# Where the conversions of w2 stand in the queues: raw slices fetched two mixing steps sooner, conversions at even distances

## The chip, the core and the metric

The kernel runs on one core of one Trainium2 chip. The time is the device time of one execution in microseconds, and the median of several runs is what is compared. A core has engines that each run their own queue of instructions in order: TensorE (PE, with PEld for its weight loads), VectorE (DVE), ScalarE (ACT), GpSimd (POOL), and SyncE (SP), which only issues transfers here.

## What is computed

The reference is an attention block, whose output goes through a Fourier mixing block:

```python
# attention: 4 batches, 8 heads, 768 tokens, head size 64
q_bucket = sum of (q @ proj > 0) bits times powers of two      # 6 bits
k_bucket = the same of k
scores = q @ k^T / 8, where q_bucket == k_bucket, else -1e9
attn = softmax(scores) @ v
# bridge: x[b, s, h*64 + d], 4 x 768 x 512
mixed = real(fft(fft(x, axis=1), axis=2))
u  = x + mixed
un = (u - mean(u)) / sqrt(var(u) + 1e-6)
out = u + relu(un @ w_ch1) @ w_ch2          # 512 -> 2048 -> 512
```

The two weight matrices come as 64-bit floats. The kernel fetches them as raw 64-bit words and makes 32-bit floats of them itself: for w_ch2 (w2 below) this is the conversion that the change moves.

## The kernel before

**Stages.** For each batch b the loop at line 1536 interleaves two generators. `attention(b)` yields once for each of its 24 chunks (4 pairs of heads, 6 chunks of 128 keys). `other` is `mix(b-1)`, the Fourier mixing and the two-layer network (`mlp7`) of the batch before, in steps that are handed out evenly between the chunks. So in the second round (b = 1) the mixing and network of batch 0 run beside the attention of batch 1.

**Attention, per chunk.** TensorE makes scores of two heads (`scores`, L894). ScalarE takes the exponential (`weights`, L905) into one of two buffers pk0 and pk1. VectorE multiplies by the bucket mask (`weigh`, L919, one instruction for each head). TensorE multiplies by the values (`values`, L930); VectorE adds the chunk into a running sum (L1007). At a pair's end come the reciprocal of the sum and the scaling (`scale`, L941 to L970). The next pair is prepared in between (`prepare`: L768, L825, L829, L839, L849).

**Mixing.** `fold`, then products with cosine and sine tables (L1122, copied by ScalarE at L1129 and L1135), then products A and B (L1151) that VectorE adds into x (L1165).

**Network.** Both layers use a scheme of seven products for eight. `quarters(f)` forms four sums and differences of a quarter of w1 in the tile tq on VectorE (L1224 to L1227) and stores the parts to DRAM (`ad`, L1229 and L1230, on SyncE) for the later batches. `inner` runs the seven products of each of eight f (TensorE, L1426); each product's bank goes through a ScalarE copy (L1448, L1451, L1458, L1463, L1467, L1475) or an activation, and a VectorE addition (L1452, L1459, L1464, L1468, L1476). Two halves of four f each are followed by a down-projection each (`outer7`, L1306).

**Conversion of w2.** w2 comes in 16 slices of 512 KB. `weights2` (L1249) fetches and converts them. There are two buffers for raw slices, in a tile (`zraw2`) that takes the place of the mixing's z. `Arrival.fetch` issues a transfer on GpSimd's queue (L693). `Arrival.convert` calls `narrow`, and then fetches the slice after next. One conversion is L639 and L643 on VectorE, L647 on ScalarE (these read the raw slice), the additions (L649, shown as L652 in the profile) on VectorE, and L654 and L655 on ScalarE, which record unusual values. After every second conversion VectorE makes four differences (L1272 to L1275). The finished half is stored to DRAM (`bd`, L1277, on SyncE).

**What sets the order.** The first round is recorded in the order written (`manual_schedule`, L1517). After it, a scheduler places the instructions on each engine's queue. It takes the traced order as priority, together with what it holds to be ready when; a `behind()` block pins some matmuls behind others. Where a conversion is called in the generators is therefore a wish, and its place in each queue is the scheduler's. A queue is run in order: an instruction that waits for a transfer holds all behind it on the same engine.

**Where the conversions are called.** `after(n, one, two)` (L1499) advances `weights2` in three of five steps of `mix(0)` from step 8 on (L1582). In the second half `mlp7` advances it at L1487 in three of four steps.

Of the kernel before, what the change touches and what calls it, by code (L numbers as in the profile page):

```python
# [17 lines left out]
ALU = mybir.AluOpType  # L18
# [467 lines left out]
def _main(  # L486
# [188 lines left out]
    def centre(f, avg):  # L675
        for c in range(NDC):
            w = w1[:, c, f : f + WC]
            nc.vector.tensor_tensor(w, w, avg, op=ALU.subtract)

    class Arrival:  # L680

# [221 lines left out]
    def weights(pk, g, ps):  # L903

        nc.scalar.activation(  # L905
            pk[:, g, :, 0:HALF], ps[:, :, 0:HALF], AF.Exp, scale=SCALE
        )

    def weigh(n, c, pss):

        qb, kb = preps[n][2:]
        pk = pks[npk[0] % NPK]
        npk[0] += 1
        for g in range(2) if n >= TWO else ():
            weights(pk, g, pss[g])
        if kb is not None:
            for h in range(2):
                w = pk[:, :, h, 0:HALF]
                nc.vector.scalar_tensor_tensor(  # L919
                    w, qb[:, h].rearrange("p (g s) -> p g s", g=2), kb[:, h, c : c + 1], w,  # L920
                    op0=ALU.is_equal, op1=ALU.mult,
                )
        return pk
# [181 lines left out]
    def mix(b):  # L1105
# [8 lines left out]
        for par in range(2):  # L1114
            for t in range(NT // 2):
# [12 lines left out]
                for k in kinds:  # L1128
                    nc.scalar.copy(  # L1129
                        f[:, k, k : hd + 1 - k],  # L1130
                        ps[:, k * (hd + 1) : DM if k else hd + 1],
                    )
# [12 lines left out]
        for j in range(NDC):  # L1145
# [10 lines left out]
            for ps, op in (pa, ALU.add), (pb, ALU.subtract):  # L1156
                for i in range(2):
# [4 lines left out]
                    else:  # L1162
                        f = ps[:, HW : HALF + 1]
                        f = bass.AP(f.tensor, f.offset, [f.ap[0], [HW, 2], [-1, HW]])
                    nc.vector.tensor_tensor(  # L1165
                        u, u, f, op=op if (j < 2) ^ i else ALU.add
# [82 lines left out]
    def weights2():  # L1249
# [14 lines left out]
        for half in range(2):  # L1264
            for i in range(arrival.depth) if half == 0 else ():
                arrival.fetch(i)
            for i in range(HF):
                arrival.convert(half * HF + i)
                yield
# [99 lines left out]
    def mlp7(b):  # L1369
# [7 lines left out]
        if b == 0:  # L1377
# [11 lines left out]
            ss = [s1s[0], spare[3].rearrange("p (r n) -> p r n", n=P)]  # L1389
            quarters(0)  # L1390
        prods = [A11, S2, A12, S1, S3, S4, A22]
# [41 lines left out]
        def inner(half):  # L1433
            for r in range(HF // 2):
# [15 lines left out]
                product(S2, p6)  # L1450
                nc.scalar.copy(c21, p6)  # L1451
                nc.vector.tensor_tensor(c21, c12, c21, op=ALU.add)  # L1452
                yield
# [3 lines left out]
                product(S1, p5)  # L1457
                nc.scalar.copy(c22, p5)  # L1458
                nc.vector.tensor_tensor(c22, c21, c22, op=ALU.add)  # L1459
                yield  # L1460
# [6 lines left out]
                nc.scalar.copy(c12, p5)  # L1467
                nc.vector.tensor_tensor(c12, c21, c12, op=ALU.add)  # L1468
                nc.scalar.activation(c12, c12, AF.Relu)
                if b and f == 0:  # L1470
# [4 lines left out]
                nc.scalar.copy(sd[1], p7)  # L1475
                nc.vector.tensor_tensor(c21, c21, sd[1], op=ALU.add)  # L1476
                nc.scalar.activation(c21, c21, AF.Relu)
                if b == 0 and r < HF // 2 - 1:
# [36 lines left out]

    ET = mybir.EngineType
    with tc.manual_schedule(engines={ET.PE, ET.DVE, ET.Activation, ET.Pool, ET.SP}):  # L1517
# [18 lines left out]
    for b in range(B):  # L1536
# [93 lines left out]
```

## Time and profile before

| what | value |
|---|---|
| median of 3 runs | 1095.56 us (1094.76 to 1096.2) |
| the profiled execution's own time | 1097.14 us |
| its span | 1095.2 us |
| TensorE busy | 1036.7 us, 95% |
| VectorE busy | 789.0 us, 72% |
| ScalarE busy | 500.1 us, 46% |
| GpSimd busy | 58.3 us, 5% |
| fetches of raw slices of w2 | 16, from 151.2 to 337.5 us |
| conversions of w2 on VectorE | from 155.8 to 346.9 us |

Times in the profile count from the span's start. In a timeline, a row is a start, a duration, engine, line, operation, tiles and shapes, and in brackets the idle time before it and what ended it. The rows overlap a little, as the engines are pipelined, so the distance from one start to the next is what an instruction takes in a row of its like. In the list of waits, the three numbers are the total, the number of times and the longest, in us.

### The profile page before, as it was taken

The numbers are of one execution on the slowest core, as the hardware profiler recorded it, in microseconds if no ns is written. First come the engines' busy times: TensorE is split into PE (matmuls) and PEld (weight loads), VectorE is DVE, ScalarE is ACT, GpSimd is POOL, SyncE is SP. The second block draws the span as 40 slices with busy tenths as digits, with TensorE's granted clock in tenths as the row PEclk, the third lists the DMA queues.
The fourth block names the chain that finished last, engine by engine and source line by source line (L and its number), as shares of the span: only waits on it lengthen the run. The fifth ranks groups of instructions, "written<-read, shape, count | busy, mean of one in ns | idle before, by whom it ended". The sixth has DMA issues, their size and how long they took to land.

```text
span 1095.2 us, 14139 instructions
## 1 busy us (share of the span) xinstructions
PE 1036.7 (95%) x4933; PEld 634.0 (58%) x4933; DVE 789.0 (72%) x1336; ACT 500.1 (46%) x1055; POOL 58.3 (5%) x132
## 2 busy tenths in 40 slices
PE   6989897999989999999999999999999999999997
PEld 3333354446744675545674576645675569768676
DVE  5899968868599978694867776876775875744353
ACT  6988555653276325364426423354415522341430
POOL 0000000002000020010000011001000002100000
PEclk9999899999999999999999999999999999999999
DMA  8744363441056162214063224213123204122401
GB/s 222 225 91 97 60 166 85 149 148 26 20 138 200 55 199 56 51 54 92 15 176 90 63 54 168 44 34 90 27 71 122 78 20 173 52 85 71 141 20 41
DMA packets 175710, 103.13 MB, mean 94 GB/s; under 512 B 129552, under 2 KB 162960, under 8 KB 175632
## 3 DMA queue, kind: packets, MB, share of 16 engines
q1 hardware_dynamic: 169840, 88.65, 30.1%
q0 software_dynamic: 4224, 13.11, 3.8%
q8 instruction: 41, 0.67, 0.3%
q10 hardware_dynamic: 1568, 0.39, 0.2%
q14 instruction: 37, 0.30, 0.1%
HBM read 81.14 MB, written 20.97 MB: 93 GB/s over the span
## 4 chain that ended last, share of the span: by engine, by line
PE 57%; DVE 15%; ACT 4%; issue 3%; DMA 2%; DVEq 0%; ACTq 0%
PE o L1306 23%; PE h_p L1426 18%; PE oo L930 5%; PE sc L894 5%; DVE pk L919 5%; DVE acc L1007 3%; PE cs L1122 2%; DMA zraw<-in_moe_w_ch_dram 2%; PE A L1151 1%; ACT rr L965 1%; ACT pk L905 1%; PE B L1151 1%; PE bits L825 1%; DVE x L1165 1%; DVE w L1318 0%
## 5 line engine op out<-in xcount | busy, mean ns | idle before, releaser
L1306 PE MATMUL o<-w,h 128*128 128x256 f32 x1152 | 258.5, 381 | 1.9 <-DVE w L1318 0.8
L1306 PEld LDWEIGHTS o<-w,h 128*128 128x128 f32 x1152 | 216.8, 190 | 41.7 <-issue 3.5
L905 ACT ACTIVATE pk<-sc 128x768 f32<-128x768 f32 x192 | 146.9, 809 | 94.2 <-PE sc L894 31.3
L1426 PE MATMUL h_p<-x,w 128*128 128x384 f32 x448 | 162.4, 492 | 2.1 <-ACT h L1448 1.7
L894 PE MATMUL sc<-qt,kt 64*128 64x384 f32 x768 | 154.2, 504 | 6.2 <-ACT pk L905 5.9
L919 DVE SCALAR_TENSOR_TENSOR pk<-qb,kb,pk 128x768 f32<-128x768 bf16 x132 | 129.3, 1012 | 34.5 <-ACT pk L905 34.3
L930 PE MATMUL oo<-pk,vn 128*64 128x385 f32 (+1 forms) x768 | 147.8, 495 | 4.9 <-DVE pk L919 4.6
L1426 PEld LDWEIGHTS h_p<-x,w 128*128 128x128 f32 x448 | 82.5, 190 | 67.2 <-issue 6.8
L1007 DVE TENSOR_TENSOR acc<-acc,pk 128x1536 f32<-128x1536 f32 (+1 forms) x72 | 105.9, 1484 | 5.9 <-ACT pk L905 5.4
L1426 PE MATMUL h_p<-w 128*128 128x384 f32 x288 | 106.3, 492 | 3.6 <-ACT w L1463 2.3
L930 PEld LDWEIGHTS oo<-pk,vn 128*64 128x64 f32 x768 | 50.7, 136 | 92.3 <-issue 73.3
L894 PEld LDWEIGHTS sc<-qt,kt 64*128 64x128 f32 x768 | 66.6, 187 | 57.4 <-issue 19.0
L1426 PEld LDWEIGHTS h_p<-w 128*128 128x128 f32 x288 | 53.0, 190 | 45.5 <-ACT w L1475 5.1
L1318 DVE SCALAR_TENSOR_TENSOR w<-o,rs,w 128x256 f32<-128x256 f32 x56 | 26.7, 479 | 42.0 <-PE o L1306 42.0
L1336 ACT COPY tq<-o 128x256 f32<-128x256 f32 x24 | 8.9, 373 | 101.8 <-PE o L1306 101.8
L1306 PE MATMUL o<-w 128*128 128x256 f32 x176 | 42.0, 381 | 0.3 <-DVE w L1318 0.3
L1459 DVE TENSOR_TENSOR h<-h 128x384 f32<-128x384 f32 x32 | 17.7, 553 | 29.5 <-ACT h L1458 29.5
L1452 DVE TENSOR_TENSOR h<-h 128x384 f32<-128x384 f32 x32 | 17.8, 555 | 26.9 <-ACT h L1451 26.8
L1306 PEld LDWEIGHTS o<-w 128*128 128x128 f32 x176 | 33.0, 190 | 6.8 <-issue 1.1
L1060 POOL DMA_DIRECT2D out_dram<-w x30 | 16.4, 548 | 376.0 <-ACT tq L1336 146.3
L1325 ACT COPY tq<-o 128x256 f32<-128x256 f32 x24 | 8.9, 370 | 58.4 <-PE o L1306 58.3
L1352 DVE TENSOR_TENSOR tq<-tq,o 128x256 f32<-128x256 f32 x24 | 10.0, 418 | 33.7 <-PE o L1306 33.7
(170 smaller groups left out, 1339.1 us busy)
## 6 DMA issues: line engine op xcount, KB each, us to landing
w<-ad SPq DMA_DIRECT2D x168, 128.0 KB, 2.0
w<-bd SPq DMA_DIRECT2D x42, 512.0 KB, 4.5
zraw<-in_moe_w_ch_dram POOLq DMA_DIRECT2D x16, 512.0 KB, 4.0
bd<-w SPq DMA_DIRECT2D x14, 512.0 KB, 4.2
vn<-in_v_dram SPq DMA_DIRECT2D x32, 192.0 KB, 3.5
qn<-in_q_dram SPq DMA_DIRECT2D x120, 48.0 KB, 2.3
kn<-in_k_dram SPq DMA_DIRECT2D x60, 96.0 KB, 3.1
zraw<-in_moe_w_ch_dram SPq DMA_DIRECT2D x8, 512.0 KB, 6.0
```

The lines of the kernel that those rows point to most:

```text
L894: last[0] = nc.tensor.matmul(ps[:, h, 0:HALF], kt[rows, ks], qt[rows, qs], start=kb is not None, stop=True,)
L905: nc.scalar.activation(pk[:, g, :, 0:HALF], ps[:, :, 0:HALF], AF.Exp, scale=SCALE)
L919: nc.vector.scalar_tensor_tensor(w, qb[:, h].rearrange("p (g s) -> p g s", g=2), kb[:, h, c : c + 1], w, op0=ALU.is_equal, op1=ALU.mult,)
L930: oo = nc.tensor.matmul(oos[g][h * D : (h + 1) * D, 0:w], nat["v", n][:, (2 * c + h) * D : (2 * c + h + 1) * D], pk[:, g, h, 0:w], start=( ...
L1007: nc.vector.tensor_tensor(acc[:, g], (first if c == 1 else acc)[:, g], new[:, g], op=ALU.add,)
L1122: nc.tensor.matmul(ps[:, pc + 2 * lo : pc + 2 * hi - 1 : 2], z[:, cp, pc, par, t * P : (t + 1) * P], ch[:, cp, pc, lo:hi], start=(cp == 0) ...
L1151: nc.tensor.matmul(ps[:, cols], F[:, par, k, t, j * P : (j + 1) * P], sq[:, t, k, cols], start=(t == 0), stop=(t == 1),)
L1306: nc.tensor.matmul(ps, a[:, r], right7[i][:, r], start=start and r == 0, stop=r == HF // 2 - 1, skip_group_check=not start,)
L1318: nc.vector.scalar_tensor_tensor(t[:, cols], src, r, t[:, cols], op0=ALU.mult, op1=ALU.add)
L1426: nc.tensor.matmul(ps, left[:, k], right[i][:, k], start=start and k == 0, stop=k == 1, skip_group_check=not start,)
L1452: nc.vector.tensor_tensor(c21, c12, c21, op=ALU.add)
L1459: nc.vector.tensor_tensor(c22, c21, c22, op=ALU.add)
```

## The change

Four edits:

- `Arrival`'s first two fetches are a step of their own, with a `yield` behind them, and the generator starts at step 6 of `mix(0)` instead of 8 (`after(NT, ...)`). The first conversion is still called at step 8.
- Conversions are called every second step of `mix(0)` (before: three in five), and in two of three steps of the second half (before: three of four).
- A dictionary `done_by` records the newest exponential, bank copy, mask or bank addition on ScalarE and on VectorE. The new context `in_turn()` queues what is traced inside it behind these, on their own engine, by order alone and with no wait for them to finish. Each conversion is wrapped in it. Nothing is pinned on GpSimd or SyncE.
- `quarters(0)` is wrapped in `in_turn()` too.

```diff
+    ET = mybir.EngineType
+    done_by = {}
+
+    @contextmanager
+    def in_turn():
+
+        with ExitStack() as st:
+            for ins in done_by.values():
+                st.enter_context(tc.issue_after(ins.ins))
+            yield
...
-        nc.scalar.activation(
+        done_by[ET.Activation] = nc.scalar.activation(
             pk[:, g, :, 0:HALF], ps[:, :, 0:HALF], AF.Exp, scale=SCALE
         )
...
-                nc.vector.scalar_tensor_tensor(
+                done_by[ET.DVE] = nc.vector.scalar_tensor_tensor(
                     w, qb[:, h].rearrange("p (g s) -> p g s", g=2), kb[:, h, c : c + 1], w,
...
-                    nc.scalar.copy(
+                    done_by[ET.Activation] = nc.scalar.copy(
                         f[:, k, k : hd + 1 - k],
...
-                    nc.vector.tensor_tensor(
+                    done_by[ET.DVE] = nc.vector.tensor_tensor(
                         u, u, f, op=op if (j < 2) ^ i else ALU.add
                     )
...
         for half in range(2):
-            for i in range(arrival.depth) if half == 0 else ():
-                arrival.fetch(i)
+            if half == 0:
+                for i in range(arrival.depth):
+                    arrival.fetch(i)
+                yield
             for i in range(HF):
-                arrival.convert(half * HF + i)
+                with in_turn():
+                    arrival.convert(half * HF + i)
                 yield
...
-            quarters(0)
+            with in_turn():
+                quarters(0)
...
-                nc.scalar.copy(c21, p6)
-                nc.vector.tensor_tensor(c21, c12, c21, op=ALU.add)
+                done_by[ET.Activation] = nc.scalar.copy(c21, p6)
+                done_by[ET.DVE] = nc.vector.tensor_tensor(c21, c12, c21, op=ALU.add)
...
-                nc.vector.tensor_tensor(c12, c21, c12, op=ALU.add)
-                nc.scalar.activation(c12, c12, AF.Relu)
+                done_by[ET.DVE] = nc.vector.tensor_tensor(c12, c21, c12, op=ALU.add)
+                done_by[ET.Activation] = nc.scalar.activation(c12, c12, AF.Relu)
...
-                if b == 0 and half and i % 4 < 3:
+                if b == 0 and half and i % 3 < 2:
                     next(arrival2, None)
...
-            if i >= n and (i - n) % 5 < 3:
+            if i >= n and (i - n) % 2 == 0:
                 next(two, None)
...
-            other = after(2 + NT, other, islice(arrival2, HF + 1))
+            other = after(NT, other, islice(arrival2, HF + 2))
```

More of the change, by code (lines that the diff above doesn't have):

```diff
@@ L1457, in inner @@
                 product(S1, p5)
-                nc.scalar.copy(c22, p5)
-                nc.vector.tensor_tensor(c22, c21, c22, op=ALU.add)
+                done_by[ET.Activation] = nc.scalar.copy(c22, p5)
+                done_by[ET.DVE] = nc.vector.tensor_tensor(c22, c21, c22, op=ALU.add)
                 yield
@@ L1475, in inner @@
                 nc.scalar.copy(sd[1], p7)
-                nc.vector.tensor_tensor(c21, c21, sd[1], op=ALU.add)
-                nc.scalar.activation(c21, c21, AF.Relu)
+                done_by[ET.DVE] = nc.vector.tensor_tensor(c21, c21, sd[1], op=ALU.add)
+                done_by[ET.Activation] = nc.scalar.activation(c21, c21, AF.Relu)
                 if b == 0 and r < HF // 2 - 1:
@@ L1513, in _main @@
     nc.sync.dma_start(sq, cn["sq"].ap())
-    ET = mybir.EngineType
     with tc.manual_schedule(engines={ET.PE, ET.DVE, ET.Activation, ET.Pool, ET.SP}):
```

## The prediction

> **What bounds the kernel now.** I read the page's busy shares first, then busy time by stretch around the change, then the list of waits, then the three engines' timelines where TensorE stands idle.
>
> ```profile
> PE 1036.7 (95%) x4933; PEld 634.0 (58%) x4933; DVE 789.0 (72%) x1336; ACT 500.1 (46%) x1055; POOL 58.3 (5%) x132
> ```
>
> TensorE is busy 1036.7 of 1095.2 us: the kernel can only gain where TensorE idles, or where its clock is low. The change touches 137 to 365 us. I cut that by what TensorE does: end of mixing, attention up to the second f of batch 0's up-projection, the rest of its first half, the first down-projection, the second half of the up-projection.
>
> ```profile
> 137.39:169.52 32.13, 29.77 (x175) 18.92 (x171) 21.91 (x39) 17.13 (x34) 2.39 (x4) 1.00 0.70 179
> 169.52:205.62 36.10, 28.78 (x114) 13.43 (x114) 30.18 (x51) 21.75 (x46) 2.12 (x4) 1.00 0.20 63
> 205.62:256.75 51.13, 46.50 (x187) 22.85 (x185) 39.31 (x71) 29.31 (x64) 2.59 (x6) 0.97 0.49 150
> 256.75:301.66 44.91, 44.58 (x220) 34.55 (x220) 32.07 (x56) 11.55 (x23) 6.06 (x9) 1.00 0.04 12
> 301.66:364.65 62.99, 58.67 (x236) 27.64 (x234) 58.43 (x113) 43.56 (x93) 2.65 (x5) 1.00 0.57 165
> ```
>
> Columns: stretch, length, busy PE, PEld, DVE, ACT, POOL, TensorE clock, DMA. TensorE's idle time is length less busy: 2.36, 7.32, 4.63, 0.33 and 4.32 us, together 18.96. In the last stretch VectorE is busy 93%, as near to full as TensorE.
>
> The list of waits, then ScalarE's timeline, tell what makes these holes:
>
> ```profile
> ACT zraw L647 <- DMA zraw<-in_moe_w_ch_dram: 23.3, 14, 4.2
> ```
>
> ```profile
> 170.73 0.67 ACT L647 ACTIVATE zraw<-zraw 128x512 int32<-128x512 uint32 x1 [3.16 <-DMA zraw<-in_moe_w_ch_dram]
> 171.31 0.79 ACT L905 ACTIVATE pk<-sc 128x768 f32<-128x768 f32 x1
> 185.07 0.68 ACT L647 ACTIVATE zraw<-zraw 128x512 int32<-128x512 uint32 x1 [1.22 <-DMA zraw<-in_moe_w_ch_dram]
> 185.65 0.79 ACT L905 ACTIVATE pk<-sc 128x768 f32<-128x768 f32 x1
> 224.08 0.67 ACT L647 ACTIVATE zraw<-zraw 128x512 int32<-128x512 uint32 x1 [2.11 <-DMA zraw<-in_moe_w_ch_dram]
> 224.63 0.78 ACT L537 CAST qb<-qb 128x768 bf16<-128x768 f32 x1
> ```
>
> The first ScalarE operation of a conversion, L647, waits for its raw slice, and the next exponential or bank copy stands behind it. TensorE then waits for that one:
>
> ```profile
> 141.31 1.16 PE L1122 MATMUL cs<-ch,z 128*128 128x127 f32 x8 [1.93 <-DVE bt L829]
> 172.15 0.92 PE L894 MATMUL sc<-qt,kt 64*128 64x384 f32 x4 [1.71 <-ACT pk L905]
> 175.98 1.51 PE L930 MATMUL oo<-pk,vn 128*64 128x385 f32 x6 [1.92 <-DVE pk L919]
> 186.49 0.92 PE L894 MATMUL sc<-qt,kt 64*128 64x384 f32 x4 [2.64 <-ACT pk L905]
> 225.47 0.24 PE L849 MATMUL kb<-pw,bt 32*128 32x2 bf16 x6 [2.10 <-ACT qb L537]
> ```
>
> The brackets hold the idle time and what ended it. The first hole is of another kind: VectorE's L829 came late behind four subtractions of `quarters(0)`:
>
> ```profile
> 137.57 0.43 DVE L1224 TENSOR_TENSOR tq<-w 128x256 f32<-128x256 f32 x1
> 138.70 0.42 DVE L1227 TENSOR_TENSOR tq<-w,tq 128x256 f32<-128x256 f32 x1
> 140.71 0.55 DVE L829 TENSOR_SCALAR bt<-bits 128x384 bf16<-128x384 f32 x1
> ```
>
> **The change part by part.** Nothing is added to or removed from the arithmetic; order alone moves. I took the new order of each engine from the built program and stepped it by hand with start-to-start durations of this trace (exponential 0.74, mask L919 0.93, sum L1007 1.65, head product L1426 1.29 per pair, score pair 0.75, values L930 1.44, conversion on VectorE 0.34+0.61+0.67 = 1.62, on ScalarE 0.6+0.6+0.8 = 2.0).
>
> *Fetch two steps sooner.* GpSimd's order is unchanged, and its first fetch (151.19) waits for the z buffer, last read by TensorE's mixing matmuls that end at 150.54. So the fetch moves only with those matmuls, about 1.5 to 2 us. Later fetches wait for L655 of the slice two before and follow the conversions. Worth nothing alone.
>
> *`quarters(0)` queued behind the newest instructions.* Its four subtractions leave 137.57 and stand at about 178. The sum at 139.04 starts at 137.57 and L829 at 139.24 instead of 140.71; its hole of 1.93 falls to 0.5. SyncE's 15 copies of w1 quarters no longer stand behind the store of tq at 139.15, and end near 141 instead of 149.8, under other work (DMA share 0.05 from 130 to 140). The small holes of 0.16 and 0.23 at 164 go too, since the masks of that chunk follow one conversion instead of two. Stretch 1: 2.36 to 0.5, gain **1.9**.
>
> *Conversions at even distances.* Before, six of eight (raw 0 to 5) sit before 197; after, two, and six in the up-projection. In stretch 2 no L647 waits for a DMA any more. What is late next: L654 of raw 1 waits for VectorE's L643 behind the third mixing add, so ScalarE stands about 4.8 us, but TensorE has score, value, sum and mixing matmuls already released. Then holes: B_3 behind the reciprocal's transpose 0.45, a score pair behind the reciprocal copies L965 1.4, first mask after `quarters(0)` 1.0. Together 2.85 against 7.32: gain **4.5**. With no cost for hand-offs the stepping gives 7; I keep the idle sum because TensorE's busy time includes split pairs that remain.
>
> *Stretch 3.* VectorE must now do six conversions from raw 2 on, where before two stood: 4 x 1.62 = 6.5 us more, into 11.82 idle (raw 2 and 3 begin just before). New hole: `quarters(1)` is done 0.85 late for the second product. L537 still stands behind an L647 (raw 6), whose slice lands just before, so 2.10 falls to 0.4. The holes at 251 and 254 (0.99, 0.94) stay. On SyncE the stores of the finished half (bd) wait for the last subtraction, about 228 on the old clock, and the next pair's queries stand behind four of them: 4 x 1.3 (six took 7.78 at 215) is 5 us, under the time to their first reader (L750 at 246.47); without that cover ScalarE would stand as long. Idle 4.63 to 3.2: gain 1.4. Then the clock:
>
> ```profile
> 222.00:226.00 4.00, 1.90 (x11) 1.01 (x11) 1.84 (x5) 1.72 (x3) 0.00 (x0) 1.00 1.03 415
> 226.00:230.00 4.00, 4.00 (x8) 2.04 (x7) 2.03 (x5) 1.53 (x3) 0.00 (x0) 0.57 0.42 159
> ```
>
> After the 2.10 us hole the granted clock was 0.57 for 4 us, which costs 4 x 0.43 = 1.7. The Trainium skill ("TensorE: Matmul & The Clock Gate", Part 1) says that the clock halves after an idle window of about 3.4 us; a 2.10 us hole should not do it, and the 2.64 us one at 184 did not (clock 1.00 after it). By the rule this dip is not due to the hole and the stretch gains 1.4; by the row it goes with the hole and gains 3.1. Since holes of up to 1.4 remain, I take half: **2.3**.
>
> *Stretch 4.* No conversion between the last down-projection products; the hole of 0.33 goes: **0.3**.
>
> *Stretch 5.* Raw 8 and 9, converted before at 291 to 302 and prepared on ScalarE at 215 and 224, now join the six others: 3.2 us more on VectorE and 4 on ScalarE, where VectorE has 4.56 idle. The hole of 1.29 (tq L1225) goes, since the quarters now run before the masks; that of 1.54 falls to 0.5. New: bank copy L1463 behind L654 of raw 10 1.65, L1451 behind L655 of raw 12 1.55, several of 0.3 to 0.6. Idle 4.95 against 4.32, plus 0.5 where the down-projection's first sum comes late: a loss of 1.1; the same stepping taken start to start gives 61.4 against 63.0, a gain of 1.6. I take **0**.
>
> A rule that speaks against it: "SBUF — State Buffer" (Who interferes with whom) says that a DMA issued by GpSimd starves for descriptors while VectorE runs a two-port operation, about 3.1 us instead of 0.62. Raw slices are such DMAs, and in stretch 5 four of them land within 1 us of their L647. By the rule each could be 2.5 late: up to 4 x 2 = 8 us lost. The row: 16 issues of 530 ns, at most 767, landing in 4.0 (median) beside a VectorE busy 93%. I take the row, 0.
>
> Sum: 1.9 + 4.5 + 2.3 + 0.3 + 0 = 9.0. The profiled execution took 1097.14 (span 1095.2 plus 1.94 around it); 1097.14 - 9.0 = 1088.1. The median of the runs shown is 1.58 below that execution: **1086.5**. About 0.2% (2.2 us) is what a measurement here can tell from no change.
>
> **The rivals.**
> 1. *Stretch 5 eats most of it.* VectorE needs 58.4 + 4.6 (conversions and their four subtractions) = 63.0; at the 94% that it reached from 310 to 350 this takes 67, 4 us more than now, and the sum is 5: 1090.5. For it: 93% is already high. Against: part of that busy time belongs to the next stage and can slide into the down-projection, VectorE 71% there.
> 2. *Hand-offs cost nothing and no clock dip returns.* 1.9 + 7 + 3.1 + 0.3 + 1.6 = 14: 1081.5.
> 3. *The change does not do what it says.* If the fetch were what matters, nothing moves, as its release stays: 1095.5. Against it: seven L647 waits lie between 160 and 225 and all get later places.
> 4. *Slower: L654 in ScalarE's queue.* It waits for VectorE's L643 of its slice, and the bank copies behind it hold TensorE. Fourteen conversions lie in the two halves of the up-projection; two of them cost 3.2 us in the sum. At 1.0 us for each of the other twelve: 1086.5 + 12 = **1098.5**. It decides from 9.0/12 = 0.75 us each. For it: L654 waited for L643 9 times before, 6.6 us, 0.73 each. Against: hardly any of those reached TensorE.
>
> **How the numbers follow.** Main case 0.62, its own range 1083.5 to 1090; rival 1 0.20; rival 2 0.06; rival 3 0.05; rival 4 0.07. Faster by over 0.2%: 0.62 + 0.20 + 0.06 = 0.88; within: 0.05; slower: 0.07. The range runs from rival 2 to beyond rival 1, 1081.5 to 1092.5; rivals 3 and 4 stay out.
>
> **What would show it.** Right: L647's 23.3 us of DMA waits fall below 6; the TensorE hole at 139 shrinks below 1; idle in the 36.10 us stretch falls by over 4; the second product of the second f waits 0.5 to 1 for tq. The dip to 0.57 gone, or elsewhere, decides the clock. Wrong: L654 or L655 named ahead of bank copies with over 1 us each, VectorE over 96% in stretch 5, or raw slices landing later than 4.5 us.

## The result, and the profile after

The changed kernel takes 1086.48 us, the median of six runs (1085.82 to 1087.07), where the kernel before takes 1095.41 (1093.39 to 1096.81). The ratio is 0.9913, with an interval of 0.9900 to 0.9926. The profiled execution took 1086.06 us, with a span of 1084.1. A second measurement of the same kernel, beside two of the experiments, gave 1087.67 against 1097.55, a ratio of 0.9915 (0.9902 to 0.9929).

The engines' busy time on the page of the changed kernel:

```profile
PE 1031.2 (95%) x4933; PEld 632.1 (58%) x4933; DVE 789.7 (73%) x1336; ACT 497.8 (46%) x1055; POOL 58.3 (5%) x132
```

The work is the same, and TensorE's busy time is 5.5 us lower. Of that, 1.6 us lie in the stretches that the change touches and are part of its gain. Another 3.7 us lie ahead of them, most of it where the kernel before ran 6.8 us at half clock and the changed kernel did not. The next fence is busy time by stretch of the changed kernel, cut at the same matmuls as in the prediction, with one row more: the opening of the second down-projection, up to the next sum over keys (L960). Most line numbers are 11 to 15 higher than before (L894 is L905, L905 is L916, L919 is L930, L930 is L941, L1426 is L1441, L1463 is L1478). Columns as in the prediction.

```profile
135.60:164.86 29.26, 28.60 (x175) 18.77 (x171) 19.77 (x28) 16.41 (x33) 1.86 (x3) 1.00 0.58 138
164.86:195.40 30.54, 27.16 (x113) 13.32 (x113) 26.86 (x46) 14.92 (x33) 0.65 (x2) 1.00 0.11 35
195.40:245.11 49.71, 46.34 (x187) 22.11 (x186) 45.38 (x88) 34.00 (x75) 4.59 (x10) 1.00 0.69 199
245.11:289.71 44.60, 44.60 (x219) 34.38 (x219) 29.52 (x49) 10.33 (x20) 5.45 (x8) 1.00 0.00 1
289.71:352.38 62.67, 59.67 (x236) 27.80 (x234) 59.80 (x114) 45.40 (x96) 3.27 (x6) 1.00 0.56 171
352.38:371.11 18.73, 17.49 (x86) 11.88 (x80) 18.73 (x38) 4.88 (x11) 0.55 (x1) 1.00 0.08 27
```

The last row's counterpart in the kernel before:

```profile
364.65:382.07 17.42, 17.13 (x86) 11.96 (x81) 17.42 (x32) 4.10 (x9) 0.55 (x1) 1.00 0.05 16
```

The five stretches are shorter by 2.87, 5.56, 1.42, 0.31 and 0.32 us, together 10.48, and the opening is longer by 1.31. That leaves 9.17. The spans differ by 11.1: 1.79 us of the rest lie ahead of 137 us, where the change does nothing, and 0.14 behind. Of the 1.79, 1.16 are there by 28 us, and the rest comes between 118 and 134, around the half clock of the kernel before (more on that under the clock).

The list of waits of the changed kernel, for the two operations that hold ScalarE's queue:

```profile
ACT zraw L654 <- DVE w L643: 10.8, 7, 4.9
ACT zraw L647 <- DMA zraw<-in_moe_w_ch_dram: 4.1, 2, 2.6
```

L647 waited 23.3 us for slices before, in 14 places; now 4.1 in two, for the first two slices, near 153 us, where TensorE has score products released already. L654 waits more than before (6.6 us). TensorE's timeline of the changed kernel has these holes where the prediction expected old ones to shrink or new ones to come:

```profile
138.25 1.16 PE L1133 MATMUL cs<-ch,z 128*128 128x127 f32 x8 [0.66 <-DVE bt L840]
173.05 0.92 PE L905 MATMUL sc<-qt,kt 64*128 64x384 f32 x4 [0.65 <-ACT pk L916]
175.43 0.92 PE L905 MATMUL sc<-qt,kt 64*128 64x384 f32 x4 [1.09 <-ACT pk L916]
179.59 1.50 PE L941 MATMUL oo<-pk,vn 128*64 128x385 f32 x4 [0.94 <-DVE pk L930]
197.82 1.53 PE L1441 MATMUL h_p<-bt,tq 128*128 128x384 f32 x4 [0.87 <-DVE tq L1236]
235.67 2.23 PE L941 MATMUL oo<-pk,vn 128*64 128x385 f32 x8 [0.23 <-PE sc L905]
320.19 1.56 PE L1441 MATMUL h_p<-zraw,w 128*128 128x384 f32 x4 [1.67 <-ACT w L1478]
329.27 1.56 PE L1441 MATMUL h_p<-bt,tq 128*128 128x384 f32 x4 [0.52 <-ACT h L1466]
355.00 3.82 PE L1320 MATMUL o<-w,h 128*128 128x256 f32 x16 [0.63 <-ACT w L1490]
359.43 1.99 PE L1320 MATMUL o<-w 128*128 128x256 f32 x8 [0.61 <-DVE w L1332]
```

The holes of 1.71, 1.92 and 2.64 behind conversions are gone, and so is the 2.10 behind L537. The hole at the cosine products went from 1.93 to 0.66.

### The profile page after: what moved, and what is told of

The parts are those of the page before. It is cut to its first block, busy times and chain, and to the rows that moved or that the text cites. A ratio compares the mean times of both kernels' runs of the same rounds, so it can differ in the third digit from the quotient of the medians.

```text
span 1084.1 us, 14127 instructions
## 1 busy us (share of the span) xinstructions
PE 1031.2 (95%) x4933; PEld 632.1 (58%) x4933; DVE 789.7 (73%) x1336; ACT 497.8 (46%) x1055; POOL 58.3 (5%) x132
## 4 chain that ended last, share of the span: by engine, by line
PE 63%; DVE 23%; ACT 6%; issue 4%; DMA 2%; SPq 2%; DVEq 0%; ACTq 0%
PE o L1320 24%; PE h_p L1441 18%; PE oo L941 7%; PE sc L905 6%; DVE pk L930 5%; DVE acc L1018 4%; PE cs L1133 2%; PE A L1162 1%; ACT pk L916 1%; ACT rr L976 1%; PE B L1162 1%; DMA kn<-in_k_dram 1%; SPq L576 1%; DVE qt L779 1%; DVE x L1176 1%
## 5 line engine op out<-in xcount | busy, mean ns | idle before, releaser
L916 ACT ACTIVATE pk<-sc 128x768 f32<-128x768 f32 x192 | 146.9, 809 | 97.3 <-PE sc L905 31.4
L1441 PE MATMUL h_p<-x,w 128*128 128x384 f32 x448 | 162.3, 492 | 0.1
L905 PE MATMUL sc<-qt,kt 64*128 64x384 f32 x768 | 153.4, 502 | 3.6 <-ACT pk L916 3.3
L930 DVE SCALAR_TENSOR_TENSOR pk<-qb,kb,pk 128x768 f32<-128x768 bf16 x132 | 128.9, 1011 | 33.7 <-ACT pk L916 33.4
L941 PE MATMUL oo<-pk,vn 128*64 128x385 f32 (+1 forms) x768 | 147.6, 495 | 4.0 <-DVE pk L930 3.4
L1441 PEld LDWEIGHTS h_p<-x,w 128*128 128x128 f32 x448 | 82.6, 190 | 64.2 <-issue 7.7
L1441 PE MATMUL h_p<-w 128*128 128x384 f32 x288 | 106.3, 492 | 3.5 <-ACT w L1478 2.3
L941 PEld LDWEIGHTS oo<-pk,vn 128*64 128x64 f32 x768 | 50.7, 136 | 90.8 <-issue 73.5
L905 PEld LDWEIGHTS sc<-qt,kt 64*128 64x128 f32 x768 | 66.4, 186 | 54.8 <-issue 18.8
L1441 PEld LDWEIGHTS h_p<-w 128*128 128x128 f32 x288 | 53.0, 190 | 45.5 <-ACT w L1490 5.1
```

The source lines that it names most:

```text
L905: last[0] = nc.tensor.matmul(ps[:, h, 0:HALF], kt[rows, ks], qt[rows, qs], start=kb is not None, stop=True,)
L916: done_by[ET.Activation] = nc.scalar.activation(pk[:, g, :, 0:HALF], ps[:, :, 0:HALF], AF.Exp, scale=SCALE)
L930: done_by[ET.DVE] = nc.vector.scalar_tensor_tensor(w, qb[:, h].rearrange("p (g s) -> p g s", g=2), kb[:, h, c : c + 1], w, op0=ALU.is_equa ...
L941: oo = nc.tensor.matmul(oos[g][h * D : (h + 1) * D, 0:w], nat["v", n][:, (2 * c + h) * D : (2 * c + h + 1) * D], pk[:, g, h, 0:w], start=( ...
L1441: nc.tensor.matmul(ps, left[:, k], right[i][:, k], start=start and k == 0, stop=k == 1, skip_group_check=not start,)
```

## The experiments

The kernel before was slower in the other measurements than in the first, 1096.6 to 1097.9 us, so a variant is read by its ratio to it, and by its median against others of the same measurement. The table also has the length of the stretches in each variant's profile, taken from the starts of the same matmuls (S6 is the opening), and L647's waits for DMA. A profile is of one execution: that of act_only is of its fastest run of nine, that of after_again of its slowest of six, and that of spacing_only is 2.8 us under its median.

| kernel | us | ratio, interval | S1 | S2 | S3 | S4 | S5 | S6 | L647's DMA waits |
|---|---|---|---|---|---|---|---|---|---|
| before | 1095.41 | 1 | 32.13 | 36.10 | 51.13 | 44.91 | 62.99 | 17.42 | 23.3 |
| changed | 1086.48 | 0.9913 (0.9900 to 0.9926) | 29.26 | 30.54 | 49.71 | 44.60 | 62.67 | 18.73 | 4.1 |
| order_only | 1089.66 | 0.9921 (0.9900 to 0.9942) | 29.25 | 32.63 | 48.47 | 44.40 | 67.81 | 16.86 | 5.4 |
| spacing_only | 1100.38 | 1.0022 (1.0010 to 1.0033) | 32.24 | 33.78 | 51.46 | 44.90 | 66.35 | 16.86 | 23.0 |
| q0_free | 1086.87 | 0.9892 (0.9873 to 0.9911) | 30.53 | 30.05 | 48.31 | 44.28 | 62.71 | 18.75 | 3.5 |
| fetch_late | 1086.93 | 0.9890 (0.9871 to 0.9909) | 29.25 | 30.55 | 50.06 | 44.60 | 62.67 | 18.74 | 3.6 |
| act_only | 1091.78 | 0.9947 (0.9930 to 0.9963) | 31.52 | 30.28 | 50.44 | 44.40 | 63.55 | 18.47 | 3.2 |
| dve_only | 1095.19 | 0.9989 (0.9979 to 0.9999) | 29.25 | 29.07 | 55.01 | 44.40 | 69.34 | 17.62 | 19.5 |
| first_half | 1092.74 | 0.9965 (0.9954 to 0.9975) | 29.26 | 31.11 | 51.80 | 45.11 | 67.85 | 16.86 | 14.2 |
| no_strange | 1086.28 | 0.9904 (0.9869 to 0.9939) | 29.25 | 31.12 | 49.03 | 44.60 | 62.28 | 17.92 | 3.3 |
| split | 1086.46 | 0.9908 (0.9873 to 0.9943) | 29.26 | 30.54 | 48.93 | 44.29 | 62.85 | 18.22 | 4.4 |
| after_again | 1087.67 | 0.9915 (0.9902 to 0.9929) | 29.25 | 31.03 | 49.68 | 44.59 | 62.68 | 18.75 | 3.5 |
| light_vector | 1087.64 | 0.9920 (0.9902 to 0.9937) | 29.26 | 30.54 | 49.70 | 44.60 | 61.49 | 18.85 | 4.0 |
| pool_diff | 1093.62 | 0.9968 (0.9960 to 0.9976) | 29.25 | 29.74 | 52.00 | 44.60 | 65.33 | 19.88 | 7.6 |

**Four variants measured together: order_only, spacing_only, q0_free and fetch_late.**

*The order without the spacing.*

```diff
                     arrival.fetch(i)
-                yield
...
-            if i >= n and (i - n) % 2 == 0:
+            if i >= n and (i - n) % 5 < 3:
...
-                if b == 0 and half and i % 3 < 2:
+                if b == 0 and half and i % 4 < 3:
...
-            other = after(NT, other, islice(arrival2, HF + 2))
+            other = after(2 + NT, other, islice(arrival2, HF + 1))
```

> The change with its in_turn() alone: conversions and quarters(0) queued behind the newest exponential, mask or bank copy, but called at the old steps (three in five of mix(0), three in four of the second half), the first two fetches at step 8 again. My theory: the gain has two parts. Queueing quarters(0) late is worth 1.9 us by itself, and the rest of the gain, about 7 us, needs both that a conversion stands behind the exponential that TensorE waits for and that its raw slice has had time to land, which the old spacing does not give. So here 1.9 plus some 2 us for the order: 1091.5 us, ScalarE's L647 still waiting over 8 us for DMA. Rival A, order is all: 1087 to 1088, L647's DMA waits below 6. Rival B, spacing is all: 1093.5, the 1.9 alone.

Measured: 1089.66 us against 1086.93 for the changed order of fetch_late, and 1097.9 for the kernel before. So 8.2 of the 11.0 us of this measurement come with the order alone; my theory had expected 4. L647's waits of 5.4 us are as in rival A. The first four stretches are as short as with the whole change (154.75 us against 154.11). What the spacing adds lies in the second half, S5: 67.81 instead of 62.67, of which the opening gives back 1.87. There conversions follow each other closely, and with them the differences. ScalarE's and then VectorE's timeline of order_only:

```profile
307.07 0.80 ACT L916 ACTIVATE pk<-sc 128x768 f32<-128x768 f32 x1
```

```profile
308.28 0.43 DVE L639 TENSOR_SCALAR w<-zraw 128x512 int32<-128x512 int32 x1 [0.34 <-DMA zraw<-in_moe_w_ch_dram]
308.62 0.42 DVE L1288 TENSOR_TENSOR w<-w 128x256 f32<-128x256 f32 x1
308.96 0.69 DVE L643 SCALAR_TENSOR_TENSOR w<-zraw,w 128x512 int32<-128x512 int32 x1
309.56 1.01 DVE L930 SCALAR_TENSOR_TENSOR pk<-qb,kb,pk 128x768 f32<-128x768 bf16 x1
```

and TensorE's:

```profile
310.83 0.83 PE L941 MATMUL oo<-pk,vn 128*64 128x385 f32 x2 [1.99 <-ACT zraw L654]
```

The exponential ends at 307.87, and the mask L930 could follow. Ahead of it stand L639, a difference and L643. L639 waits 0.34 us for its slice, and the three take 1.28, so the mask starts at 309.56 and ends at 310.57, and the values product starts at 310.83. The row names L654, but what ended just before it is the mask. Pinning a conversion behind the newest work does not protect the next mask from it: here more by the conversion's own length than by the wait for its slice. Of the 5.14 us, up to 1.7 come from 3.41 us at half clock from 333.65 on, behind holes of 1.70 and 0.92; that need not come in every execution.

*The spacing without the order.*

```diff
-            for ins in done_by.values():
+            for ins in ():
                 st.enter_context(tc.issue_after(ins.ins))
```

> The change without in_turn(): the even distances and the earlier fetch stay, the places in the queues are the scheduler's again, for quarters(0) too. My theory: the scheduler places several ScalarE conversions ahead of exponentials before their slices have landed, so L647's DMA waits stay above 10 us, and the hole of 1.9 us at the cosine product behind L840 comes back: 1092 to 1094 us. Rival A, order is all: 1095.5. Rival B, spacing is all: 1088.5, the changed kernel plus the 1.9 of quarters(0).

Measured: 1100.38 us, a little slower than before (ratio 1.0022). All three expectations missed, mine by 6 us, or by 4 when it is allowed for that the kernel before took 1097.9 here and not 1095.4. The list of waits of this kernel has the line of the kernel before almost unchanged:

```profile
ACT zraw L647 <- DMA zraw<-in_moe_w_ch_dram: 23.0, 12, 4.2
```

Calling a conversion later does not place it later: without a pin the scheduler put L647 ahead of exponentials and bank copies again. In the second half TensorE has a hole of 3.92 us behind a bank copy, L1463, which stands behind an L647 that waited 2.48 us, two exponentials, the reciprocal copies, L654 and L655.

*quarters(0) left where it was.*

```diff
-            with in_turn():
-                quarters(0)
+            quarters(0)
```

> The changed kernel with quarters(0) outside in_turn(): its four subtractions go back in front of the sum and L840 on VectorE, near 136 us. My first step of the sum: the hole in front of the second half of the cosine products grows from 0.66 to about 1.9, while the mask that waited 0.94 near 179 us no longer waits behind the four: minus 1.4 here and plus 1.0 there would nearly cancel, but my sum took 1.9 for the stretch, so 1088.0 us (1087.5 to 1088.5). Rival: the two cancel, 1086.5 to 1087.

Measured: 1086.87, the same as fetch_late's 1086.93. The rival was right. TensorE's timeline of q0_free:

```profile
140.48 1.16 PE L1133 MATMUL cs<-ch,z 128*128 128x127 f32 x8 [1.92 <-DVE bt L840]
207.48 0.52 PE L836 MATMUL bits<-qt,pj 128*32 128x384 f32 x2 [1.12 <-ACT h L1481]
```

The hole at the cosine products is back at 1.92, and a new one of 1.12 comes; but the wait of 0.87 for tq is gone, and the first mask of the later chunk holds TensorE 0.48 instead of 0.94. In the stretches: S1 1.27 longer, S2 and S3 0.49 and 1.40 shorter. Queueing quarters(0) late moved its price from 140 us to 180 and 198; it did not save it.

*The fetch back in its old step.*

```diff
                     arrival.fetch(i)
-                yield
...
-            other = after(NT, other, islice(arrival2, HF + 2))
+            other = after(2 + NT, other, islice(arrival2, HF + 1))
```

> The changed kernel with the first two fetches called together with the first conversion again, at step 8 instead of 6. The program that comes out has the same instructions in the same order on all five queues. My theory and rival 3's first half: the fetch is worth nothing, 1086.5 us, within 0.3; the profile is a second sample of the changed kernel. Rival: the fetch carries some of the gain through a due time that the order does not show, over 1087.5.

Measured: 1086.93. The first fetch waits for the z buffer in either case. The two mixing steps are worth nothing, and the profile is a second sample of the changed order: S1, S2, S4, S5 and the opening repeat within 0.02 us, S3 within 0.35.

**Four more, measured together: no_strange, split, first_half and act_only.**

*Without L654 and L655.*

```diff
+        if col >= NDC * DFF // WC:
+            return
         nc.scalar.activation(t, hi, AF.Abs)
```

> The changed kernel without L654 and L655 for w2's sixteen slices: the look for unusual values is left out for w2, the conversion itself stays. My theory for what is left of TensorE's idle time: L654 waits on ScalarE for VectorE's L643, and bank copies and exponentials stand behind it. The holes of the changed kernel that I put down to this are 1.67 and 0.52 (behind L1478 and L1466 in the second half), 0.36, 0.63 at the second down-projection's start, and part of 0.65 and 1.09 (exponentials near 174): 3 to 4 us, so 1083 to 1084 us. Rival: VectorE, 95% busy in the second half, is what holds; then ScalarE's two operations hide and it stays at 1086 to 1087.

This leaves out the recording of unusual values for w2. Measured: 1086.28, against 1086.46 for split in the same measurement, and at a ratio like that of the whole change. S5 and the opening went from 81.40 to 80.20; my 3 to 4 us are refuted. The holes 1.67 and 0.36 went, but others came: TensorE waits 2.25 us before the product at 335.96. ScalarE's and then VectorE's timeline of no_strange ahead of it:

```profile
335.02 0.52 ACT L1482 ACTIVATE h<-h 128x384 f32<-128x384 f32 x1 [3.32 <-DVE h L1481]
335.45 0.46 ACT L1484 COPY h<-h_p 128x384 f32<-128x384 f32 x1
```

```profile
329.88 1.76 DVE L1020 TENSOR_TENSOR acc<-acc,pk 128x1536 f32<-128x1536 f32 x1
331.55 0.55 DVE L1469 TENSOR_TENSOR h<-h 128x384 f32<-128x384 f32 x1
332.69 0.69 DVE L643 SCALAR_TENSOR_TENSOR w<-zraw,w 128x512 int32<-128x512 int32 x1
333.76 0.75 DVE L652 CUSTOM_DVE_ANT_0 w<-zraw,w 128x512 uint16<-128x512 uint16 x2
334.44 0.55 DVE L1481 TENSOR_TENSOR h<-h,w 128x384 f32<-128x384 f32 x1
```

(Lines here are two higher than in the changed kernel, and three rows of VectorE are left out.) VectorE works without a gap; ScalarE's activation waits for the addition L1481, and the copy that TensorE needs stands behind it.

*L654 and L655 one step later.*

```diff
                 with in_turn():
-                    arrival.convert(half * HF + i)
+                    rest = arrival.convert(half * HF + i)
+                yield
+                with in_turn():
+                    rest()
+                    arrival.fetch(half * HF + i + arrival.depth)
                 yield
...
-            if i >= n and (i - n) % 2 == 0:
+            if i >= n and (i - n) != 1:
...
-                if b == 0 and half and i % 3 < 2:
-                    next(arrival2, None)
+                if b == 0 and half:
+                    for _ in range(1 + (i in (1, 3, 5, 7))):
+                        next(arrival2, None)
```

> The changed kernel with L654, L655 and the next fetch as a step of their own, one step after the rest of the conversion, both queued behind the newest exponential or bank copy; in the second half 18 steps are handed out over 14. L654 then stands behind one more bank copy, when L643 has run. Theory (L654 in ScalarE's queue costs 2 to 3 us in the second half): 1084.5 us. Rival 1 (VectorE's load holds): 1086.5. Rival 2 (the fetch, now later by a step, makes L647 wait for its slice again): over 1088.

Measured: 1086.46, no gain (rival 1). L654's waits for L643 fell from 10.8 us to 7.0; S5 is 0.18 longer and the opening 0.51 shorter.

*The order in the first half alone.*

```diff
-                with in_turn():
+                with in_turn() if half == 0 else ExitStack():
                     arrival.convert(half * HF + i)
```

> The changed kernel with in_turn() only around the first eight conversions and quarters(0); in the second half the new spacing stays and the scheduler places the conversions. The runs so far: second half with the start of its down-projection took 80.41 us before, 81.40 after, 84.67 with the order at the old spacing, 83.21 with the spacing alone. Theory: the order costs in the second half what its bank copies lose behind L654, about 1 us, and a free scheduler gives that back: 1085.5. Rival: free placement brings waits for DMA back, as where the spacing stood alone (a hole of 3.92): 1088.5.

Measured: 1092.74, so the rival, and by more than it said. ScalarE's timeline of first_half:

```profile
227.50 0.45 ACT L1473 COPY h<-h_p 128x384 f32<-128x384 f32 x1
231.95 0.66 ACT L647 ACTIVATE zraw<-zraw 128x512 int32<-128x512 uint32 x1 [4.00 <-DMA zraw<-in_moe_w_ch_dram]
232.51 0.46 ACT L1478 COPY w<-h_p 128x384 f32<-128x384 f32 x1
```

and TensorE's:

```profile
233.02 1.56 PE L1441 MATMUL h_p<-zraw,w 128*128 128x384 f32 x4 [2.53 <-ACT w L1478]
```

This is the whole mechanism in four rows. L647 of an unpinned slice stands in the queue ahead of a bank copy, waits 4.00 us for the transfer, the copy follows at once, and TensorE has stood 2.53 us for it.

*The pin on one engine alone (act_only here, dve_only in a later measurement).*

```diff
-            for ins in done_by.values():
+            for e, ins in done_by.items():
+                if e != ET.Activation:
+                    continue
                 st.enter_context(tc.issue_after(ins.ins))
```

> The changed kernel with in_turn() pinning ScalarE's instructions alone; VectorE's part of a conversion and quarters(0) go where the scheduler puts them. My theory: the exponential behind L647 is the chain that costs, but L654 needs L643 on VectorE, so both engines have to be in step: half of the order's gain of 10 us, 1091 us. Rival A, ScalarE's queue is all: 1087. Rival B, VectorE's place is all: 1096.

> The changed kernel with in_turn() pinning VectorE's instructions alone (the conversions' and quarters(0)); ScalarE's part of a conversion goes where the scheduler puts it. With the order on ScalarE alone the run took 1091.8 against 1096.6 before, about half of the gain. Theory: what costs is L647 standing with its wait for the slice ahead of exponentials and bank copies; without a pin on ScalarE its DMA waits come back to 10 us or more, and the time is 1094 to 1097, the other half of the gain being had only with both. Rival: the halves add, 1091 to 1092, VectorE's masks being as much of it as ScalarE's queue.

(dve_only has ET.DVE in that line.) Measured: 1091.78 against 1096.55 with the pin on ScalarE, 1095.19 against 1097.18 with the pin on VectorE. Both theories held in size; that of dve_only is barely clear of no change (ratio 0.9989, 0.9979 to 0.9999). The waits are, in act_only and then in dve_only:

```profile
ACT zraw L647 <- DMA zraw<-in_moe_w_ch_dram: 3.2, 2, 2.4
```

```profile
ACT zraw L647 <- DMA zraw<-in_moe_w_ch_dram: 19.5, 13, 3.3
```

The pin on ScalarE takes the waits away, and brings about half of the gain. The rest needs VectorE's pin too, but that pin by itself is worth 2 us.

**The last three, measured together: after_again, light_vector and pool_diff.**

*The changed kernel once more.*

> The changed kernel, as it is, beside the other two on the same chip: what they are compared with. 1086.5 us, within 0.5; if it repeats, the three profiles of this order (this one, the first, and the one with the fetch back in its old step) show what of a stretch repeats and what does not.

Measured: 1087.67 (1086.54 to 1089.35), 0.7 over the expected band. The stretches repeat, except S2, by 0.5; that is the clock, below.

*Less work for VectorE.*

```diff
+        if not NDC * DFF // WC + HF <= col < 2 * NDC * DFF // WC:
             nc.vector.tensor_scalar(
                 di, hi, 3, (1 << 30) - 1,
...
             nc.vector.scalar_tensor_tensor(
```

> The changed kernel without L639 and L643 for the eight slices of the second half: what they compute of those slices is left out, L647, L652, L654, L655 and all transfers stay. It takes 8 x (0.34 + 0.61) = 7.6 us off VectorE between 290 and 352 us, and L654 has nothing on VectorE to wait for. Without L654 and L655 nothing was gained, so my theory now is that VectorE's load, 95% there, is what is left: second half with the start of its down-projection from 81.4 to 77.5 us, 1083 us in all. Rival: the bank copies' order on ScalarE or the slices' landing hold: 1086 us.

This leaves out what L639 and L643 compute of those eight slices. Measured: 1087.64, the same as after_again. With 7.6 us less for VectorE (6.9 of its busy time in S5), S5 and the opening are 80.34 instead of 81.40. So the load as such is not what holds there either: my second theory fell as well. What stayed is the end. VectorE's timeline of the changed kernel where TensorE waits at 355.00 and 359.43:

```profile
353.94 1.02 DVE L1098 TENSOR_TENSOR ef<-ef 128x384 f32<-128x384 f32 x2
354.88 0.95 DVE L535 CAST qb<-qb 128x768 bf16<-128x768 f32 x1
355.75 1.15 DVE L1107 TENSOR_TENSOR z<-ef 128x190 f32<-128x190 f32 x4
356.97 0.55 DVE L1491 TENSOR_TENSOR h<-h,w 128x384 f32<-128x384 f32 x1
358.90 0.48 DVE L1332 SCALAR_TENSOR_TENSOR w<-o,rs,w 128x256 f32<-128x256 f32 x1
```

The last addition of the layer, L1491, stands behind work for the next batch's mixing (L1098, L1107). In light_vector the same instructions stand in the same order, and the same holes follow, 0.75 and 0.61. Where S5 took 66 to 68 us (order_only, spacing_only, first_half) the opening has neither hole and takes 16.86, so the two are not independent. No run moved these two instructions alone, so that they are the cause of the last microsecond is only argued.

*The differences on GpSimd.*

```diff
-                    nc.vector.tensor_tensor(t3, b22, t1, op=ALU.subtract)
-                    nc.vector.tensor_tensor(t1, t1, b11, op=ALU.subtract)
-                    nc.vector.tensor_tensor(t2, b22, t1, op=ALU.subtract)
-                    nc.vector.tensor_tensor(t4, b21, t2, op=ALU.subtract)
+                    nc.gpsimd.tensor_tensor(t3, b22, t1, op=ALU.subtract)
+                    nc.gpsimd.tensor_tensor(t1, t1, b11, op=ALU.subtract)
+                    nc.gpsimd.tensor_tensor(t2, b22, t1, op=ALU.subtract)
+                    nc.gpsimd.tensor_tensor(t4, b21, t2, op=ALU.subtract)
```

> The changed kernel with the four differences after every second conversion (L1286 to L1289) on GpSimd instead of VectorE, in both halves. VectorE sheds 16 x 0.34 = 5.4 us in each half; GpSimd is busy 6.5 us in 89 us of the two up-projections. Theory (VectorE's load holds the second half): 81.4 to 79 us there, some 0.5 in the first half, 1083.5 us, faster than both kernels. Rival 1: VectorE and GpSimd slow each other down while both run, and what VectorE sheds it loses to longer instructions: 1086.5. Rival 2: the fetches stand behind the differences on GpSimd's queue, slices land late and L647 waits again: over 1088.

Measured: 1093.62 against 1087.67. Both rivals at once. GpSimd's timeline, the slowest place, of pool_diff:

```profile
338.41 4.86 POOL L1286 TENSOR_TENSOR w<-w 128x256 f32<-128x256 f32 x1 [4.70 <-DVE w L652]
343.35 0.73 POOL L1287 TENSOR_TENSOR w<-w 128x256 f32<-128x256 f32 x1
344.02 0.56 POOL L704 DMA_DIRECT2D zraw<-in_moe_w_ch_dram  x1
```

A subtraction takes 0.73 us in its quickest places; the first one here takes 4.94 from start to start, and the next fetch stands behind the second. VectorE worked without a gap from before that until 342.68, almost all of it in operations with two inputs. VectorE's masks in S5, in pool_diff and then in the changed kernel (busy time and mean ns behind the bar):

```profile
L930 DVE SCALAR_TENSOR_TENSOR pk<-qb,kb,pk 128x768 f32<-128x768 bf16 x12 | 13.9, 1202 | 3.1 <-ACT pk L916 3.0
```

```profile
L930 DVE SCALAR_TENSOR_TENSOR pk<-qb,kb,pk 128x768 f32<-128x768 bf16 x12 | 11.7, 1007 | 0.0
```

Twelve masks cost 2.2 us more, and of the 5.4 us that VectorE shed in S5 only 1.2 show in its busy time (58.64 us instead of 59.82). The Trainium skill ("SBUF — State Buffer", Who interferes with whom) says that VectorE's operations with two inputs in SBUF and GpSimd's reads share an interface, and that whoever holds it blocks the other; the rows agree in both directions. How much of the loss is this and how much the fetches (L647 waits 7.6 us, in four places) was not separated. No variant beat the changed kernel by more than the measurement tells.

## Why the prediction came out right

The mechanism was right: L647's waits fell, and most of the gain lies where they stood. The total was right too, 9.17 us in the stretches against 9.0 in the sum, but the terms were not all of the right size. Two were too small by 1 us each, two too large by 0.9 and 1.0, and that these cancel is luck.

**Cause.** "L647 waits for its raw slice, and the next exponential or bank copy stands behind it" is shown by first_half's rows, and by the table: where L647's DMA waits stay at 14 to 23 us the ratio is 0.9965 or more, and with 3 to 5.4 us, apart from act_only's 0.9947, it is 0.989 to 0.992. act_only also shows the limit of it: without the waits, but with VectorE's part of the conversions unpinned, half of the gain is missing (its quarters(0) is unpinned too, which by itself costs nothing, as q0_free shows). pool_diff (7.6) has a second cause of its own.

**Fetch two steps sooner**, worth nothing: right (fetch_late).

**quarters(0)**: the hole fell as worked out, 1.93 to 0.66 (forecast 0.5), and the new waits came, 0.94 for the first mask (1.0) and 0.87 for tq (0.85). Since the sum had entered those in stretches 2 and 3, its net gain was none, as measured. Calling it 1.9 in my expectations of order_only and q0_free counted one side.

**Stretches 1 and 2**: 1.9 and 4.5 forecast, 2.87 and 5.56 measured. The term that failed is "I keep the idle sum because TensorE's busy time includes split pairs that remain". Much of it did not remain: idle time fell by 1.70 and 3.94, and busy time by 1.17 and 1.62 more. In stretch 2 the stepping start to start (7) was too high by 1.4, the idle sum too low by 1.1. The holes themselves were placed well: 1.4 forecast at the score pairs, 1.09 and 0.65 found.

**Stretch 3**: 2.3 forecast, 1.42 measured. The dip to 0.57 did not come, which gives the full 1.7, not half. One term was too small: the wait for tq costs 1.13 from start to start, not 0.85. Another was missing: at 235.67 the values product starts 0.3 late and takes 2.23 us instead of 1.51. Its masks begin 1.90 us after the sum's product, before 0.84, since VectorE runs behind, 45.38 busy us in 49.71.

**Stretch 4**: 0.3, right.

**Stretch 5**: 0 forecast. It gained 0.32, and the opening lost 1.31, so 1.0 was lost. L1478 (old L1463) behind L654 cost 1.67 (forecast 1.65). The old L1451 behind L655 cost 0.52 instead of 1.55. What was sized too small is "0.5 where the down-projection's first sum comes late". Rival 1, that this stretch gives back 4, did not come. A loss of that size is in the profile without the spacing (order_only: 84.67 to 80.41, 4.3), but up to 1.7 of it is the half clock there. The reason that rival 1 gave, VectorE's load, is not supported: 7.6 us less of it brought 1.1 (light_vector).

**Rival 4**, L654 in ScalarE's queue at 0.75 or more for each of twelve conversions: excluded. Taking L654 and L655 away altogether gains 1.2 in stretch 5 and the opening, 0.1 each. Waits of L654 on ScalarE rose to 10.8 us, but only one of them reached TensorE with over 1 us, the 1.67; so one of the named signs of being wrong was seen, once.

**Rival 3**, that the change does not do what it says, was right for the fetch and for the spacing alone, and wrong for the order. I had not separated these in the prediction: I wrote of "conversions at even distances" as what takes the waits away. It is the queue's order that does it, 8.2 of 11.0 us.

**Start**: 1.58 us were taken off because the profiled execution stood that much above the median of the runs shown. That execution had a dip of the clock ahead of 137 us, and its first 137 us were 1.79 slower than the changed kernel's. But in the later measurements, 23 to 28 runs each, the median of the kernel before is 1096.6 to 1097.9, so that 1097.14 was not a slow execution; and the gain there is 9.9 (after_again) to 11.0 (fetch_late), where the first measurement has 8.9. That the forecast met 1086.48 to a tenth is luck; 9 to 11 us of gain is what the runs show.

**Signs**: idle time in stretch 2 fell by 3.94 where over 4 was named. VectorE stayed below the 96% that would have spoken against it (59.80 of 62.67, 95.4%). The slices land in 4.3 us (median) beside it, so the rule of starvation that I weighed and set to 0 did not show. Its two figures, 3.1 us and 0.62, stand in the same page of the Trainium skill, but in the section "A bandwidth-pool intuition that's wrong (but worth ruling out)", and for a copy on VectorE, not for the operations of this kernel.

## What to carry to other kernels

An instruction that waits for a transfer on a queue that feeds the bottleneck is priced here by what stood behind it, not by its length: queue it behind the newest instruction that the bottleneck waits for, on every engine that it uses. Calling it later in the program is not enough where a scheduler places it; look at the built order. And once the order is right, space the calls, since a pinned conversion, with its length and what is left of its wait, still stands ahead of the next mask.

## What was not expected of the hardware

**The clock follows fixed windows.** In the clock records of the fourteen traces the granted clock is full or half, and within a trace it changes at whole multiples of 3.413 us. In dve_only, for example, it falls to half at 117.95, 179.39, 227.18, 319.34 and 339.82, which are 18, 14, 27 and 6 such windows apart. (The 0.57 that the prediction read is 3.41 us at half clock, seen through a cut of 4.) The kernel before, cut at its own windows, around its holes of 2.64 and 2.10 us:

```profile
181.88:185.29 3.41, 1.95 (x11) 0.93 (x11) 2.10 (x4) 2.11 (x10) 0.00 (x0) 1.00 0.44 159
185.29:188.71 3.42, 2.22 (x13) 1.32 (x15) 2.94 (x4) 3.42 (x7) 0.00 (x0) 1.00 0.00 0
222.84:226.25 3.41, 1.31 (x10) 0.72 (x9) 1.25 (x4) 1.72 (x3) 0.00 (x0) 1.00 1.03 413
226.25:229.66 3.41, 3.41 (x6) 1.66 (x6) 1.78 (x4) 1.48 (x3) 0.00 (x0) 0.50 0.31 122
```

The hole of 2.64 lies across two windows, with 1.46 and 1.20 us idle in them, and nothing follows. That of 2.10 lies in one, and the next window runs at half clock. I counted all 4359 windows at full clock up to each trace's last matmul. TensorE was idle for 2.0 us or more in 11, and a half-clock window followed every one. It was idle for 1.6 to 2.0 us in 44, and one followed 9 of them; what decides there was not found. It was idle for less in 4304, and none followed.

So the dip at 226 goes with its hole, and the whole 1.7 us with it; half was too little. The same holes can bring a dip in one execution and not in another, as the windows fall. The changed order has holes of 0.65 and 1.09 us near 175, and so have seven of the variants. In no_strange, first_half and after_again both lie in one window (1.61 to 1.71 idle) and the clock fell; in the other five profiles no window there had over 1.46, and it did not. The changed kernel, and then its repetition, which runs 2.9 us later there:

```profile
172.97:176.38 3.41, 2.23 (x11) 0.91 (x12) 2.94 (x6) 3.01 (x11) 0.00 (x0) 1.00 0.03 7
```

```profile
174.80:178.21 3.41, 1.80 (x10) 0.73 (x8) 2.94 (x8) 3.00 (x11) 0.00 (x0) 1.00 0.19 73
178.21:181.62 3.41, 3.27 (x12) 1.87 (x14) 3.41 (x8) 2.19 (x5) 0.00 (x0) 0.50 0.01 2
```

It costs 0.5 us of S2. Two holes of 1.61 and 1.51 ahead of 118 us do the same: in seven profiles, that of the kernel before among them, one window there was idle for 1.85 to 2.35 us and the clock fell; in the other seven, the first of the changed kernel among them, none was idle for over 1.7. The Trainium skill ("TensorE: Matmul & The Clock Gate", Part 1) gives an idle window of about 3.4 us and calls it free-running. Length and free running agree with these records; that a whole window must be idle does not, since 2.0 us of 3.4 were enough.

**Waits for transfers may spread the time.** With the order the runs lie within 1.2 us (changed, six runs) and 2.8 (after_again, six); where L647 waits in the queue, within 6.4 (the kernel before, 23 runs), 7.4 (dve_only, 20) and 8.4 (spacing_only, 20). first_half does not fit: its L647 waits 14.2 us, and its 20 runs lie within 3.9. The numbers of runs differ too, and the six runs of the kernel before in the first measurement lie within 3.4, so this is an observation; that the transfers' own spread reaches TensorE through ScalarE's queue was not tested.
